# Attention and long-convolution kernel: projection tails in row halves, q begun with the second token quarter, x spectra by thirds

## The chip, the cores and the metric

The kernel runs on one NeuronCore of a Trainium2 chip. Its engines are TensorE (PE; its weight loads are PEld), VectorE (DVE), ScalarE (ACT), GpSimd (POOL) and SyncE (SP), which here only starts DMA transfers. The metric is the device time of one execution in microseconds (us); lower is better. Time before: 226.44 us, the median of 3 runs (225.37 to 228.72).

## What is computed

Two independent blocks whose results stand side by side in the last dimension of the output; S is 2048 tokens, D is 576.

```python
# A: 32 heads of 18, each token looks at 8 keys: itself and those 2, 4, ... 14 tokens back
q, k, v = split(x @ wqkv)
logits = sum_d q[s] * k[s - 2 w] / sqrt(18)      # w = 0..7, masked below token 0
a = (softmax(logits) weighted sum of v[s - 2 w]) @ wo
# B: a short and a long convolution along the tokens, gated
k_shift = 4-tap causal convolution of k with shift_k
kv = k_shift * v
y = causal convolution of kv with ssm_k (length 2048, by FFT) + kv * ssm_D
b = q * y
out = concatenate([a, b], -1)
```

## The kernel before

All operations are put in a list under short names, with a function that issues each one. A long text, ORDER, gives each operation's place in the program and, for those that need it, one of four accumulator slots of 1024 columns. Each engine works off its own instructions in that order, and so do the DMA queues of SP, ACT and POOL. Nothing is reordered at run time: an instruction that waits holds up all that its engine has behind it.

Block A. `load_x` brings x in four token quarters, turned so that channels lie on partitions: `x0`, `x2`, `x3` (channels 0 to 511, in four blocks of 128) and `xt0`, `xt2`, `xt3` (the last 64 channels) by a transposing DMA on SP (L187). Quarter 1 is loaded plainly (`xn`), turned on PE (`nx0` to `nx2`, L299) and copied out (`nx0e`, `nx1e` on ACT, L304; `nx2e` on VectorE, L305). `load_w` brings the weights of q, k and v (comp 0, 1, 2): `w0` to `w2`, four blocks of 128 rows, and `wt0` to `wt2`, the last 64 rows, which lie on partitions 64 to 127 under 64 rows of zeros that `constants` writes (L205). `hot0` and `hot1` are warm-up products (L313).

`project` makes unit `p{comp}{ct}{hh}`: component, channel tile 0 to 4 and token half hh. For q and k with ct below 4 a unit is ten full 128x128 products of 512 columns at L402: two token quarters by five row blocks, the fifth being the 64 rows and the 64 zeros. For v each product is split in two column halves that run side by side, ten pairs. The last tile (ct 4, 64 channels, L415) is five pairs. Each unit's result is copied by ACT (`...e`, L406 or L419).

Behind that come the logits products on VectorE (`l{hh}{ug}{ct}`, L442), their sums over a head on PE with 32-column pieces (`L...`, L450), the softmax (`sm...`; its Exp on ACT, L473), copies of the weights to the heads' channels by DMA on SP (`s...`, `spread`), products with v on VectorE (`w...`, L675) and their sums on PE with 32x32 pieces (`a...`, L689), and the output projection (`o...`, L735), stored by SP.

Block B. `tab...` and `sin0` to `sin3` make tables of sines (L260 to L263, after small number ranges that POOL writes in `constants`); `taps` makes the short convolution with 64x64 pieces on PE, four at a time (L501), `fold` transposes its result, and `x_spectrum(i)` makes the spectra of block i of four: units `x{i}{gi}{pm}`, L547 and L548, evicted at L616. `filter_spectrum` (`k...`, same lines, evicted at L601) does so for the filter. VectorE adds the x spectra's two parts (`S{i}`, L769) and the filter's (`W{d}`, L766), multiplies spectra (`z{j}{t}{i}`, L780), PE sums the products with 32x32 pieces (`Z...`, L804, evicted at L815 or L819), transforms back (`i{j}{t}`, L837, evicted at L841), and `gate` multiplies with q of block B (`g...`, L856, L857, L866, L870) and stores.

The order of PE's units in ORDER, from the warm-up on, up to the first unit of the second token half:

```
hot0 nx0 nx2 nx1 hot1 p030 p000 p100 p110 p010 p020 p120 L000 ti0 p130 L010 p140 p040 L011 L001 L002 p001
```

and around the start of the last part: `p231 p221 p211` are the last value projections; behind `i00`, the first transform back, three x units of block 2 and all eight of block 3 still follow.

Of the kernel before, what the change touches and what calls it, by code (L numbers as in the profile page):

```python
# [16 lines left out]
ORDER = """
1o o 1u 6 u 1c 1i 16 30 5o 4i 36 20 0 2p 120 2e 26 2u 13 2i 3u 3i 8c 5c 6o bl 3c 86 4u 8i 5i 7i 60
9k 66 6c 7o 6i 6u 3o 9u 7u bo 7c al c a0 5u 9o 1k6 a6 ao 126 i mo 56 ax ac 80 mc b6 b0 50 8o n0 ml
40 8w bv 90 nc bc mw c0 ci no 130 go c7 co ni cc cu n6 oc nu d0 d7 46 136 o0 du dc 4o oo 4c o6 e0 oi  # L20
dj pi p0 ou do po 96 16i wu p6 9c gv pc e6 146 h0 pu h6 ek q6 16o qc 13c wi ec 12p m0 eo 12c hf qi
12u 15c 70 12i iw hi 14c 17c ic j0 ho hv 76 16u ii f9 l6 io 1eu 15i qo qu eu i0 r0 176 i6 j6 17i jp
fc r6 fk rc ju ri ro f0 lu 13v fo wo x3 140 x6 je g7 ji 14i xi xc gc 13k 1fj 13o gi lo 17o xu 15o xo
1fo 14q y6 y0 14u kd 180 li k2 ki yi yc k6 fv 152 g0 yu yo lc 156 kp 18i 1f2 ku l0 18c z6 18o z0 1f6
zc zo 170 167 zi 15w 17u zu 16c so 100 1fu tp su 160 ru 1gl 190 t0 s0 186 1h0 18u 106 1go 10c 1jq
10i 1h6 10o 1hi 1g0 1hc tu 10u m6 u0 1m6 t9 1ju 110 u7 1g6 116 s8 tc 1mi 2i0 ti 1k0 1ho 1gc 1mc sc
1fc 1m0 uc ui si 19v 1hu 11c 1d3 11i 198 1d6 v0 19c ur 1a0 11o 11u vq uu vd 1mo 1l6 vu 1l0 1j9 1kc
1q6 1mu 1q0 1iq 1pu 1jc vi 1ji 1n0 1gu 1i9 v6 1iu 1n6 23o 1ic 1oc 25q 1o6 261 23u 1ii w3 1oi 266 1no
1i0 1oo 25u 1nc 1j0 w6 wc 1nx 1ni 1aw 1o0 23c 1b0 24p 1al 23i 1ce 24u 1a6 1p0 1ao 1cp 1ci 253 1ac
1c2 256 19i 1p6 1e0 1c6 273 1b6 1cu 27q 1qc 276 26p 1lc 1pc 27u 1e9 26u 1de 1ec 27d 1di 1br 1ou 27i  # L30
25e 1bu 1bd 25i 1qi 1bi 1s0 1pk 19o 1ku 1li 1lo 24c 1qo 1po 1ki 281 1ko 1si 1s6 286 1ek 1r0 1sc 243
24i 26d 1eo 1do 26i 1ze 1du 1qu 1zv 1zi 1zo 28e 200 20u 1ri 28i 206 246 1lu 20d 2io 210 1r8 20i 216
2n0 21d 1rc 1su 22c 1rq 22i 1so 21i 22o 20o 1tp 1ru 1u0 1tu 293 1t0 1vo 2ae 1u6 21o 21v 296 2ai 29r
1t6 220 1vw 29u 28p 1w0 29c 2mu 1te 28u 29i 2ii 1uo 1ti 1ud 2iu 1uu 2jo 2j2 1ui 2j6 2ki 2ju 2n6 2k0
1v2 2no 22x 1v6 2p0 2ko 230 2oi 2ku 2ne 2ni 2nu 2jc 2qc 1y7 2o0 2ji 2a2 1vf 1yc 1vi 2oo 2ou 2a6 2k9
2p6 1xk 2kc 2pc 1wu 1xv 1x0 2l3 1xo 1y0 1wk 2l6 1w6 1yi 1x7 1wc 2lc 226 2br 1xc 236 2b0 2so 2bu 2bd
2b6 1z3 2ic 2t0 2bi 1yo 1wo 2pj 2pu 1yu 1z6 2ao 2vi 2c2 2au 2cf 2i6 2c6 2o6 2su 2ci 2po 2q2 2zc 2tu
2q6 2oc 2cp 2qi 2uo 2e0 2cu 2tc 2de 2qo 2el 2di 2e6 2d2 2eo 2ec 2t6 2li 2d6 2ti 2to 2v0 2dq 2u0 2f3
2uu 2u6 2f6 2wc 2v6 2du 2fc 2vc 2eu 2qx 2wo 2vo 2gk 2x6 2r0 2vu 2lo 2lu 2r6 2m9 2g1 2m0 2mc 2ro 2zi
2mi 2fl 2g6 2go 2gc 2ru 2ud 2fo 2zu 2fu 2wk 2ui 2wu 2x0 2zo 2xc 30c 300 306 2s2 2xi 2hl 2rc 30i 2s6  # L40
2ri 30o 330 2h2 2ho 30u 2w3 2h6 32i 310 2hc 2sc 2xq 2mo 316 356 32c 2xu 32o 2w6 32u 336 2si 33c 35o
2hu 352 33i 35c 35i 2yu 2y0 35u 360 2y6 33p 366 2z0 2yc 2gu 31c 2yi 33u 31i 36e 2yo 31o 340 2z6 34i
346 36i 31v 34o 34c q0 378 36o 34u 36u 37c 370 320 37i 326
"""


# [35 lines left out]
def kernel(  # L82
# [114 lines left out]
    def constants():  # L197
        nc.vector.memset(pib[:], float(np.float32(np.pi)))
        act(warm[:], pib[:], ACT.Sin)
        nc.gpsimd.iota(rp_i[:, 0:2], pattern=[[128, 2]], base=0, channel_multiplier=1)  # L200
        nc.gpsimd.iota(rp_i[:, 2:4], pattern=[[256, 2]], base=1, channel_multiplier=2)
        for gi in range(4):
            nc.gpsimd.iota(fr_i[:, gi, :], pattern=[[16, 128]], base=4 * gi + 1, channel_multiplier=0)
# [186 lines left out]
    def project(comp, ct, hh):  # L390
        o, pad = ((qat, 0), (kat, PAD), (vat, PAD))[comp]
        o = o(ct, hh)
        box = Box()
        nm = f"p{comp}{ct}{hh}"
        if ct < 4:
            def unit():
                for jp in range(2):
                    for kb in range(5):
                        ws = wcol(comp, kb, ct)
                        for a, w in enumerate(ws):  # L400
                            p = slice(64 * a, 64 * a + 64) if len(ws) > 1 else slice(0, 128)
                            mm(box.ps[p, jp, :], w, xT(kb, 1024 * hh + 512 * (jp ^ a), 512), start=(kb == 0),  # L402
                               stop=(kb == 4), tile_position=(0, 64 * a))

            op(nm, unit, box, 1)
            op(nm + "e", lambda: act(M(o + pad, [[KH if comp == 2 else 512, 2], [1, 512]]), box.ps, ACT.Copy), box,  # L406
               free=True)
# [4 lines left out]
        def unit():
            for kb in range(5):
                for e in range(2):
                    mm(box.ps[64 * e:64 * e + 64, 0, :], wcol(comp, kb, 4)[0], xT(kb, 1024 * hh + 512 * e, 512),  # L415
                       start=(kb == 0), stop=(kb == 4), tile_position=(0, 64 * e))

        op(nm, unit, box, 1)
        op(nm + "e", lambda: act(M1(o + pad, 512), box.ps[:, 0, :], ACT.Copy), box, free=True)  # L419
        if comp:  # L420
            dma(nm + "a", M1(o, PAD)[64:128], M1(o + 512, PAD)[0:64])
# [181 lines left out]
            scale=KSC), box, free=True)  # L603

    def x_spectrum(i):
        for gi in range(4):
            for pm in range(2):
                box = Box()

                def unit(box=box, gi=gi, pm=pm):  # L610
# [4 lines left out]
                op(f"x{i}{gi}{pm}", unit, box, 1)  # L615
                op(f"x{i}{gi}{pm}e", lambda box=box, gi=gi, pm=pm: act(  # L616
                    M((BS if pm else AS) + SPB * i + TH * gi, [[4 * TH, 3], [1, TH]]), acc3(box.ps), ACT.Copy),
                   box, free=True)
# [331 lines left out]
```

## Time and profile before

| | |
|---|---|
| median of 3 runs | 226.44 us (225.37 to 228.72) |
| profiled execution | 226.6 us |
| its span, first to last instruction | 224.9 us |
| mean granted TensorE clock | 0.973 |
| PE busy | 205.2 us, 3027 products |
| VectorE busy | 178.3 us |
| ACT busy | 144.8 us |
| POOL busy | 45.9 us |

In lines of the profile, L402 is line 402 of the kernel before; `<-` stands between what is written and what is read, with partitions x elements; `[5.04 <-X]` is idle time of the engine just before, and what ended it. The large buffer in SBUF is called mem, the accumulator PS. The chain of waits is followed back from the last instruction; "issue" in it is waiting that no semaphore explains. Matmuls are pipelined, so the length of a chain piece divided by its products is their true pitch, while the mean duration of one product is longer.

### The profile page before, as it was taken

The numbers are of one execution on the slowest core, as the hardware profiler recorded it, in microseconds if no ns is written. First come the engines' busy times: TensorE is split into PE (matmuls) and PEld (weight loads), VectorE is DVE, ScalarE is ACT, GpSimd is POOL, SyncE is SP. The second block draws the span as 40 slices with busy tenths as digits, with TensorE's granted clock in tenths as the row PEclk, the third lists the DMA queues.
The fourth block names the chain that finished last, engine by engine and source line by source line (L and its number), as shares of the span: only waits on it lengthen the run. The fifth ranks groups of instructions, "written<-read, shape, count | busy, mean of one in ns | idle before, by whom it ended". The sixth has DMA issues, their size and how long they took to land.

```text
span 224.9 us, 6868 instructions
## 1 busy us (share of the span) xinstructions
PE 205.2 (91%) x3027; PEld 132.9 (59%) x3033; DVE 178.3 (79%) x147; ACT 144.8 (64%) x188; POOL 45.9 (20%) x108
## 2 busy tenths in 40 slices
PE   7379999999999999999999989996899999999590
PEld 3124444445455557678767657663687778787380
DVE  0693787988879967899749999999508999999642
ACT  2322776378794765645989876769998985645140
POOL 7929203001401084020660000000110111010000
PEclk9958999999999999999999999999999999999978
DMA  6999923569894986475541464100666749659323
GB/s 179 292 259 244 176 65 66 82 140 134 157 240 85 190 152 119 75 166 137 130 106 22 112 139 141 55 26 3 212 118 187 245 99 210 218 129 272 125 81 79
DMA packets 54150, 31.87 MB, mean 142 GB/s; under 512 B 41984, under 2 KB 51016, under 8 KB 54120
## 3 DMA queue, kind: packets, MB, share of 16 engines
q1 hardware_dynamic: 50456, 24.12, 46.9%
q0 software_dynamic: 2528, 6.06, 13.2%
q10 hardware_dynamic: 1136, 1.25, 2.0%
q8 instruction: 24, 0.39, 0.8%
q14 instruction: 6, 0.05, 0.1%
HBM read 5.68 MB, written 4.72 MB: 46 GB/s over the span
## 4 chain that ended last, share of the span: by engine, by line
PE 72%; DMA 10%; DVE 5%; ACT 5%; issue 3%; SPq 2%; DVEq 0%; ACTq 0%
PE PS L402 22%; PE PS L735 8%; PE PS L837 8%; PE PS L804 5%; PE PS L547 5%; DMA mem<-in_A_x_dram 5%; PE PS L450 5%; DMA mem<-mem 4%; PE PS L501 3%; PE PS L415 3%; DVE mem L675 3%; PE PS L548 2%; PE PS L689 2%; SPq L184 2%; PE PS L866 2%
## 5 line engine op out<-in xcount | busy, mean ns | idle before, releaser
L402 PE MATMUL PS<-mem 128*64 128x512 bf16 (+1 forms) x314 | 56.7, 392 | 5.4 <-DMA mem<-in_A_x_dram 5.0
L402 PEld LDWEIGHTS <-mem 128*128 128x128 bf16 (+1 forms) x320 | 31.1, 147 | 29.4 <-issue 11.0
L442 DVE TENSOR_TENSOR mem<-mem 128x4096 bf16<-128x4096 bf16 (+1 forms) x20 | 40.6, 2076 | 9.1 <-ACT mem L406 5.7
L675 DVE TENSOR_TENSOR mem<-mem 128x4096 bf16<-128x4096 bf16 x18 | 40.1, 2288 | 4.7 <-DMA mem<-mem 2.9
L406 ACT ACTIVATE mem<-PS 128x1024 bf16<-128x1024 f32 x24 | 24.3, 1023 | 25.3 <-PE PS L402 25.2
L780 DVE TENSOR_TENSOR mem<-mem 128x4608 bf16<-128x4608 bf16 (+3 forms) x21 | 38.1, 1868 | 1.1 <-PE PS L804 0.7
L184 POOL DMA_DIRECT2D mem<-mem x16 | 14.0, 996 | 114.5 <-ACT mem L815 61.0
L547 PE MATMUL PS<-mem 128*128 128x384 bf16 x128 | 33.4, 326 | 2.0 <-ACT mem L695 1.0
L548 PE MATMUL PS<-mem 128*128 128x192 bf16 x128 | 31.4, 246 | 0.0
L735 PE MATMUL PS<-mem 128*128 128x288 bf16 x160 | 21.7, 286 | 0.2 <-DMA mem<-in_A_wo_dram 0.2
L616 ACT ACTIVATE mem<-PS 128x576 bf16<-128x576 f32 x32 | 19.7, 661 | 0.9 <-PE PS L548 0.7
L601 ACT ACTIVATE mem<-PS 128x576 bf16<-128x576 f32 x32 | 19.7, 675 | 0.6 <-PE PS L548 0.2
L837 PE MATMUL PS<-mem 128*128 128x192 bf16 x192 | 18.8, 256 | 0.5 <-ACT mem L819 0.5
L804 PE MATMUL PS<-mem 32*32 32x384 bf16 x960 | 15.1, 328 | 3.9 <-issue 2.6
L547 PEld LDWEIGHTS <-mem 128*128 128x128 bf16 x128 | 12.5, 98 | 9.8 <-issue 1.4
L735 PEld LDWEIGHTS <-mem 128*128 128x128 bf16 x160 | 15.3, 98 | 4.7 <-issue 0.9
L837 PEld LDWEIGHTS <-mem 128*128 128x128 bf16 x192 | 16.8, 102 | 1.9 <-ACT mem L819 0.7
L740 ACT ACTIVATE mem<-PS 128x576 bf16<-128x576 f32 x16 | 10.2, 649 | 8.6 <-PE PS L735 7.7
L804 PEld LDWEIGHTS <-mem 32*32 32x32 bf16 x960 | 9.7, 88 | 9.0 <-issue 6.8
L509 DVE TENSOR_TENSOR mem<-PS,mem 128x512 bf16<-128x512 f32 (+1 forms) x20 | 11.7, 631 | 3.5 <-ACT mem L456 2.1
L548 PEld LDWEIGHTS <-mem 128*128 128x128 bf16 x128 | 12.5, 98 | 2.6 <-issue 1.9
L841 ACT ACTIVATE mem<-PS 128x768 bf16<-128x768 f32 x12 | 9.6, 817 | 5.9 <-PE PS L837 5.8
(111 smaller groups left out, 276.2 us busy)
## 6 DMA issues: line engine op xcount, KB each, us to landing
mem<-mem SPq DMA_DIRECT2D x16, 256.0 KB, 4.3
mem<-mem POOLq DMA_DIRECT2D x8, 288.0 KB, 4.0
out_dram<-mem SPq DMA_DIRECT2D x16, 144.0 KB, 2.3
mem<-mem SPq DMA_DIRECT2D x6, 384.0 KB, 3.4
mem<-mem POOLq DMA_DIRECT2D x6, 384.0 KB, 4.3
mem<-in_B_q_dram SPq DMA_DIRECT2D x4, 576.0 KB, 4.1
out_dram<-mem SPq DMA_DIRECT2D x6, 288.0 KB, 2.5
mem<-in_A_wqkv_dram POOLq DMA_DIRECT2D x2, 576.0 KB, 6.2
```

What stands on the lines that cost most here:

```text
L402: mm(box.ps[p, jp, :], w, xT(kb, 1024 * hh + 512 * (jp ^ a), 512), start=(kb == 0), stop=(kb == 4), tile_position=(0, 64 * a))
L406: op(nm + "e", lambda: act(M(o + pad, [[KH if comp == 2 else 512, 2], [1, 512]]), box.ps, ACT.Copy), box, free=True)
L442: op(f"l{hh}{ug}{ct}", lambda prod=prod, nt=nt, qo=qo, ko=ko, ug=ug: tt(M(prod, [[nt, 4], [1, nt]]), M(qo, [[0, 4], [1, nt]]), M(ko + 2 + ...
L547: mm(view(ps, 0, [[320, 2], [1, TH]]), w, rhs[:, 0:2, :], start=start, stop=stop)
L548: mm(view(ps, 640, [[1, TH]]), w, rhs[:, 2, :], start=start, stop=stop)
L601: op(f"k{m}{gi}{cs}e", lambda: act(M((VS if cs else US) + SPB * (3 - m) + TH * gi, [[4 * TH, 3], [1, TH]]), acc3(box.ps), ACT.Copy, scale= ...
L616: op(f"x{i}{gi}{pm}e", lambda box=box, gi=gi, pm=pm: act(M((BS if pm else AS) + SPB * i + TH * gi, [[4 * TH, 3], [1, TH]]), acc3(box.ps), ...
L675: op(f"w{n}{ct}", lambda: tt(M(P, [[2048, 2], [256, W], [1, 256]]), M(XB[n], [[2048, 2], [256, W], [1, 256]]), M(vo + 2, [[256, 2], [2, W] ...
L735: mm(box.ps[:, h, 0:HD], M1(lhs, 128), M1(rhs, HD), start=(i == 0), stop=(i == 4))
L780: tt(M(pr + 768 * k, [[2304, n], [768, m], [1, 768]]), M(BS + i * SPB + o + PL * k, [[SPB, n], [PL, m], [1, 768]]), M(VS + (3 - j + i) * S ...
L804: mm(view(box.ps[32 * c:32 * c + 32], box.step * (r // 2) + 512 * (r % 2), [[TH, 2], [1, TH]]), I32S[w][32 * r:32 * r + 32], M(pr + src + ...
L837: mm(box.ps[:, pm, TH * c:TH * c + TH], M1(TI + 512 * sl + 256 * pm + 128 * c, 128), M1((YT if j else YRS[0]) + 1536 * t + 768 * pm + TH * ...
```

## The change

Four things change, and ORDER is written anew with them.

1. **Tails.** The last 64 rows of the projection weights are loaded twice, to partitions 0 to 63 (`wt`) and 64 to 127 (`wu`), which adds three DMAs of 72 KB; the zeros and the memset that wrote them are gone. The last 64 channels of x lie on partitions 0 to 63 for token quarters 0 and 2 and on 64 to 127 for 1 and 3. The fifth row block of a unit is then computed by 64-row products, those of two quarters at the same time in the two row halves of the array. In q units and even v tiles the tail comes last, in k units and odd v tiles first.
2. **q first.** Each q unit of the first token half with ct below 4 is cut in two: `p0{ct}0q` makes the four full products of quarter 1, the rest makes those of quarter 0 and the tail.
3. **x spectra.** Unit `x{i}{t}{pm}` makes one third (192) of the channels for all four frequency groups, eight products of 192 columns, evicted as 128x768; before, a unit made one frequency group for all channels, two products of 384 and two of 192 columns, evicted as 128x576. 24 units instead of 32.
4. **Order.** Behind `i00` one x unit of block 2 and all six of block 3 follow. PE's units up to the second token half now are:

```
hot0 nx2 nx0 nx1 hot1 p000q p010q p030q p020q p030 p010 p000 p100 p020 p110 p040 p140 L000 L010 p120 p130 ti0 L001 L011 p001
```

Transposing DMAs on SP were `xt0 x0 vbt0 hl0 kt0 xt3 x2 k0 x3 xt2 va0` and are `xt0 x0 xt3 xt2 vb0 vat0 x3 hl0 x2 k0`. ACT's first steps were the DMAs `xn wt0 w0`, the Sin table with a small warm-up (in `const0`), `nx0e nx1e`; they are the DMAs `xn w0 wu0 wt0`, then `nx1e`, `const0`'s table and warm-up, `nx0e`. POOL's DMAs were `w1 wt2 wt1`, then the ranges of `const0`, `sh4 sh0 w2`; they are `wu1 w1 wt1 sh4 sh0`, then the ranges; `wu2 w2` stand behind `p001`'s issue and `wt2` after the first taps. ACT's use of tables was `sin0 sin2 sin3 sin1 sm0x sm1x` and is `sin3 sin2 sin0 sm0x sin1 sm1x`. On VectorE, `S2` and `z201` now stand ahead of `g00h`. On SP, `s300` now stands behind the store `o0000s`.

The diff, without ORDER:

```diff
@@ constants
-        nc.gpsimd.memset(M(WW + 4 * D, [[5 * D, 3], [1, D]])[0:64], 0.0)
@@ load_w
-        dma(f"wt{comp}", M1(b + 4 * D, D)[64:128], A_wqkv[512:576, comp * D:(comp + 1) * D], eng)
+        for a in range(2):
+            dma(f"w{'tu'[a]}{comp}", M1(b + 4 * D, D)[64 * a:64 * a + 64], A_wqkv[512:576, comp * D:(comp + 1) * D], eng)
@@ load_x
-        xbar(f"xt{qtr}", M1(X4 + 512 * qtr, 512), xf[512 * qtr:512 * qtr + 512, 448:576])
+        xbar(f"xt{qtr}", M1(X4 + 512 * qtr, 512),
+             bass.AP(tensor=xf.tensor, offset=xf.offset + 512 * qtr * D + (448 if qtr % 2 else 512), ap=[[D, 512], [1, 128]]))
@@ project
+        cols = (0,) if comp < 2 and ct < 4 else (0, 1)
+        jps = (0, 1) if ct < 4 else (0,)
+        tail_first = (comp == 1) if comp < 2 else ct % 2 == 1
+        two = comp == 0 and hh == 0 and ct < 4
+        def full(jp, first, last):
+            for kb in range(4):
+                ws = wcol(comp, kb, ct)
+                for a in cols:
+                    p = slice(64 * a, 64 * a + 64) if len(cols) > 1 else slice(0, 128)
+                    mm(box.ps[p, jp, :], ws[a % len(ws)], xT(kb, 1024 * hh + 512 * (jp ^ a), 512),
+                       start=first and kb == 0, stop=last and kb == 3, tile_position=(0, 64 * a))
+        def tails(first):
+            ws = wcol(comp, 4, ct)
+            for jp in jps:
+                for a in cols:
+                    r = jp ^ a
+                    p = slice(64 * a, 64 * a + 64) if len(cols) > 1 else slice(0, 128)
+                    mm(box.ps[p, jp, :], ws[a % len(ws)][64 * r:64 * r + 64],
+                       xT(4, 1024 * hh + 512 * r, 512)[64 * r:64 * r + 64], start=first, stop=not first,
+                       tile_position=(64 * r, 64 * a))
+        def unit():
+            if tail_first:
+                tails(True)
+            for jp in jps[:1] if two else jps:
+                full(jp, not tail_first, tail_first)
+            if not tail_first:
+                tails(False)
+        if two:
+            op(nm + "q", lambda: full(1, True, False), box, 1)
+        op(nm, unit, box, 0 if two else 1)
@@ x_spectrum
-        for gi in range(4):
+        for t in range(3):
             for pm in range(2):
...
-                    for c in range(2):
-                        mm3(box.ps, M1(TX + 1024 * c + 512 * pm + 128 * gi, 128),
-                            thirds(AB + 2304 * i + 1152 * c + 576 * pm), c == 0, c == 1)
+                    for gi in range(4):
+                        for c in range(2):
+                            mm(box.ps[:, gi // 2, TH * (gi % 2):TH * (gi % 2) + TH],
+                               M1(TX + 1024 * c + 512 * pm + 128 * gi, 128),
+                               M1(AB + 2304 * i + 1152 * c + 576 * pm + TH * t, TH), start=(c == 0), stop=(c == 1))
```

More of the change, by code (lines that the diff above doesn't have):

```diff
@@ L23 @@
[L23 to L27, printed above, removed]
@@ new lines @@
+wk w0 1mi 1kd 1mo 1r0 1oc 1lu 1lo 1jx 1ki wo 1nu 1jd 1k0 1ec 1k6 1o0 24u 1ji 1pc x9 1pi 26k 250 1jo
+1po 1ou xc 1j6 1pu 1oi xi 1ko 26o 1lc 1p2 1oo 1c3 1p6 24i 1c6 1d8 24o 25v 279 1dc 1bc 260 1q6 268
+1bi 1ap 26c 1di 1cc 27c 1dw 1q0 1mc 1f6 1do 1br 1rc 1au 27i 1ri 1e0 1cj 1qc 27o 1fe 1co 27u 1fi 287
+1qi 280 1cw 1bu 1ei 1d0 1eo 1ro 1qq 1to 28c 1m6 1mu 1m0 25j 1qu 1s0 1ti 26u 1l6 1tc 270 1ew 1s6 259
+1f0 1fo 20k 1fu 25c 1ru 210 20o 21l 20u 216 1t6 1so 220 21o 25o 21u 1se 1n0 226 2h6 21c 22c 1v6 1si
@@ L44 @@
+35u 35i 30i 360 30o
 """
@@ L394, in project @@
         nm = f"p{comp}{ct}{hh}"
-        if ct < 4:
[L396 to L405, printed above, removed]
+        cols = (0,) if comp < 2 and ct < 4 else (0, 1)
[28 more added lines that the diff above has]
+        op(nm, unit, box, 0 if two else 1)
+        if ct < 4:
             op(nm + "e", lambda: act(M(o + pad, [[KH if comp == 2 else 512, 2], [1, 512]]), box.ps, ACT.Copy), box,
@@ L410, in project @@
             return
[L412 to L418, printed above, removed]
         op(nm + "e", lambda: act(M1(o + pad, 512), box.ps[:, 0, :], ACT.Copy), box, free=True)
@@ L605, in x_spectrum, with unit @@
     def x_spectrum(i):
-        for gi in range(4):
+        for t in range(3):
             for pm in range(2):
                 box = Box()
-                def unit(box=box, gi=gi, pm=pm):
-                    for c in range(2):
-                        mm3(box.ps, M1(TX + 1024 * c + 512 * pm + 128 * gi, 128),
-                            thirds(AB + 2304 * i + 1152 * c + 576 * pm), c == 0, c == 1)
[L615 to L618, printed above, removed]
+                def unit(box=box, t=t, pm=pm):
+                    for gi in range(4):
[3 more added lines that the diff above has]
+                               M1(AB + 2304 * i + 1152 * c + 576 * pm + TH * t, TH), start=(c == 0), stop=(c == 1))
+                op(f"x{i}{t}{pm}", unit, box, 1)
+                op(f"x{i}{t}{pm}e", lambda box=box, t=t, pm=pm: act(
+                    M((BS if pm else AS) + SPB * i + 4 * TH * t, [[2 * TH, 2], [1, 2 * TH]]), box.ps[:, :, 0:2 * TH],
+                    ACT.Copy), box, free=True)
     taps(0)
```

41 lines of the change are left out of this document (20 added, 21 removed).

## The prediction

> **What bounds the kernel now.** I read the page from its head to the chain, then the table by stretches, then the order of time at the start, then the chain's pieces.
>
> ```profile
> span 224.9 us, 6868 instructions
> PE 205.2 (91%) x3027; PEld 132.9 (59%) x3033; DVE 178.3 (79%) x147; ACT 144.8 (64%) x188; POOL 45.9 (20%) x108
> PE 72%; DMA 10%; DVE 5%; ACT 5%; issue 3%; SPq 2%; DVEq 0%; ACTq 0%
> ```
>
> PE carries 72% of the chain, but not everywhere. The table by stretches (stretch, length, busy us and instruction counts of PE, PEld, DVE, ACT, POOL, then clock, DMA share, GB/s):
>
> ```profile
> 140.00:150.00 10.00, 9.80 (x102) 6.62 (x103) 10.00 (x5) 8.19 (x13) 0.00 (x0) 1.00 0.14 46
> 150.00:160.00 10.00, 7.68 (x310) 4.84 (x278) 9.14 (x8) 8.69 (x13) 0.00 (x0) 1.00 0.23 78
> 160.00:170.00 10.00, 9.69 (x151) 8.01 (x152) 2.03 (x3) 9.31 (x14) 1.77 (x2) 1.00 0.54 124
> 8.00:12.90 4.90, 0.02 (x1) 0.12 (x2) 4.74 (x7) 0.00 (x0) 3.78 (x6) 0.84 1.20 294
> 12.90:18.20 5.30, 5.25 (x12) 1.85 (x13) 5.25 (x9) 2.01 (x2) 2.15 (x4) 0.51 1.22 285
> ```
>
> From 140 to 160 VectorE is full and PE has slack; from 160 PE leads again. At the start PE is idle for 4.9 us and then works 5.3 us at half clock. The order of time there:
>
> ```profile
> 1.29 1.18 ACTq L184 DMA_DIRECT2D mem<-in_A_wqkv_dram  x2
> 2.50 1.28 ACT L199 ACT_TABLE_LOAD   x1 [2.50 <-issue]
> 3.80 0.20 ACT L199 ACTIVATE warm<-pib 128x1 f32<-128x1 f32 x1
> 5.48 1.94 ACT L304 ACTIVATE mem<-PS 128x1024 bf16<-128x1024 f32 x2 [1.48 <-PE PS L299]
> 5.95 1.89 PE L313 MATMUL PS<-mem 128*128 128x512 bf16 x8
> 8.48 0.10 PEld L402 LDWEIGHTS <-mem 128*128 128x128 bf16 x1 [1.14 <-DMA mem<-in_A_wqkv_dram]
> 12.88 17.84 PE L402 MATMUL PS<-mem 128*128 128x512 bf16 x68 [5.04 <-DMA mem<-in_A_x_dram]
> 24.09 6.70 DVE L442 TENSOR_TENSOR mem<-mem 128x4096 bf16<-128x4096 bf16 x3 [5.13 <-ACT mem L406]
> ```
>
> The q weights are there at 8.48 and token quarter 1 (turned on PE, evicted at L304) at 7.42; PE waits until 12.88 for quarter 0, which the DMA transposes. VectorE's first logits product waits for its operands until 24.09.
>
> **The change, part by part.** Lengths of chain pieces (start, us, what):
>
> ```profile
> 12.88 5.28 PE PS L402 x12
> 47.73 0.99 PE PS L501 x16
> 86.35 2.37 PE PS L402 x20
> 88.71 2.16 PE PS L415 x20
> 109.85 0.27 PE PS L547
> 111.16 5.62 DMA mem<-mem
> 161.81 0.16 PE PS L547
> 162.05 0.16 PE PS L547
> 200.77 3.96 PE PS L837 x48
> ```
>
> A turn of 512 columns takes 0.44 us cold (5.28/12) and 0.216 warm (2.16/10, since 20 half-width products run in pairs).
>
> *q with the second quarter.* The four new q pieces need 16 turns, the q weights and quarter 1, and not the transposed quarter 0. Their start is set by ACT. It issues one DMA more ahead of its first eviction, which is free (1.29 + 3 x 0.59 = 3.06, before hot1 begins at 5.95, behind the transposes), but in the new order the constants, with the Sin table, stand between the two evictions of quarter 1: 5.95 + 0.2 + 1.0 + 1.28 + 0.20 + 1.0 = 9.6 (1.0 is half of L304's two; 0.2 and a further 0.1 are handovers). So q begins near 9.75 (bounds 8.48, when weights came, and 12.88). If warm, 16 turns end at 9.75 + 3.45 = 13.2, when quarter 0 has just come: PE's useful work begins 3.1 us earlier, and the 12 turns that ran at 0.44 run at 0.216: 12 x 0.22 = 2.7 more. Gain 5.8.
>
> Does VectorE follow? Its tables wait for POOL's iotas, which now stand behind five DMA issues of POOL (the extra weight rows among them; W2's loads moved far back):
>
> ```profile
> 5.22 2.08 POOL L184 DMA_DIRECT2D mem<-in_A_wqkv_dram  x3
> 7.42 0.86 POOL L203 IOTA mem<- 128x128 int32 x4
> 9.64 1.39 POOL L184 DMA_DIRECT2D sh<-in_B_shift_k_dram  x2
> 9.92 2.11 DVE L260 TENSOR_SCALAR mem<-mem,rp 128x512 int32<-128x512 int32 x3
> 15.98 2.98 DVE L335 TENSOR_TENSOR mem<-mem,sh 64x1280 bf16<-64x1280 bf16 x2
> ```
>
> 5.22 + 2.08 + 1.39 + about 1.0 of iotas = 9.7; then the tables and the diagonals, which took 9.92 to 18.96 here and have one step more (2.11/3 = 0.7): 19.5. The memset that is removed stood behind the iotas and sets nothing. PE's operands for the first product: 13.2, then p030, p010, p000, p100 with 24 turns (5.2) and six changes of tile shape (0.8), and an eviction of 1.0: 20.2. So products begin near 20.3 instead of 24.09, 3.8 earlier, and VectorE's own idle places behind it give the rest; PE needs the second product 0.6 before it is there. I charge +0.6.
>
> *Tails in row halves.* 16 q/k units go from ten turns to nine and 8 v units from ten pairs to nine, if the halves run side by side; the five-turn units of the last channels keep five. 24 x 0.216 = 5.2 saved. Against it stand changes of tile shape: counted unit by unit in the two orders, PE passes 71 before and 104 after, since the new order puts a q unit that ends in a tail ahead of a k unit that begins with one. Price: the taps' 16 products (L501) are four turns, 0.86, and took 0.99, so 0.13 for a group; 20 half-width products took 2.37 after another shape and 2.16 beside their own, 0.21 for both ends of a group. 33 x 0.13 = 4.3. Net -0.9. Row halves on the full width have no row; the nearest are the same taps, 64x64 pieces four at a time, of which two share each column half from different row halves: 16 products in 0.99, so row halves do run together. Bounds: -5.2 if changes cost nothing; +4.3 if the halves ran one after the other. I take -0.9, by the row nearest in shape. The Trainium skill (TensorEngine Tiling, Key Properties) says that changing the tiling mode drains TensorE; the 0.13 agrees. By that page's twofold speedup alone, without the drain, the term would be -5.2 and the time some 4 lower.
>
> All this lies ahead of the last value projection (109.85). There the chain goes on by the spread of the attention weights (DMA 5.62) into VectorE, whose work from there to i00 is the same: the gain is handed on, neither more nor less. One transfer of the last spread now stands behind an output store on SP's queue, so the fourth group of products could wait: 0 to 2, I take 0.5.
>
> *x spectra in thirds.* PE before: 32 units of two pairs, a pair each 0.245 (162.05 - 161.81): 15.7. After: 192 products of 192 columns at 3.96/48 = 0.0825: 15.8. Weight loads rise by 128:
>
> ```profile
> L616 ACT ACTIVATE mem<-PS 128x576 bf16<-128x576 f32 x32 | 19.7, 661 | 0.9 <-PE PS L548 0.7
> L841 ACT ACTIVATE mem<-PS 128x768 bf16<-128x768 f32 x12 | 9.6, 817 | 5.9 <-PE PS L837 5.8
> ```
>
> They are hidden: PE loads weights for nearly each product (x3033 beside x3027), those of L837 too, and these run at 0.0825. ACT: 32 x 0.661 = 21.2 becomes 24 x 0.817 = 19.6, not on the chain. What counts is where the units stand: behind i00, where PE leads, the old order has 11 of them (5.4), the new one seven (4.6): -0.8. S2 and a product of j=2 move ahead of the gate on which VectorE idles between 160 and 170; PE leads there, so zero.
>
> *Table.* sin1 now stands between the two Exp calls, so ACT loads two tables more, 1.28 each. The first falls while PE has four tap units and two projections in hand, the second while VectorE evicts taps: 0, or 2.6 if PE or VectorE stood waiting for ACT instead.
>
> Sum: -5.8 + 0.6 - 0.9 + 0.5 - 0.8 = -6.4. The profiled execution took 226.6 (span 224.9 and 1.7 around it), the median is 226.44, so both stand for the same state: 226.6 - 6.4 = **220.2**.
>
> **The rivals.**
>
> *Cold clock (222.9).* PE is idle from 7.84 to 9.75. Near the end a 2.57 us stop was followed by half clock:
>
> ```profile
> 211.13 0.37 PE L804 MATMUL PS<-mem 32*32 32x384 bf16 x12 [2.57 <-issue]
> 213.13 2.74 PE L837 MATMUL PS<-mem 128*128 128x192 bf16 x16
> 216.37 1.48 PE L837 MATMUL PS<-mem 128*128 128x192 bf16 x16
> ```
>
> If 1.9 us is enough too, q's first turns cost 0.44 again and the 2.7 is lost. Against it: warm-up matmuls end only 1.9 before. The Trainium skill (TensorE: Matmul & The Clock Gate, Part 1) has a free-running window of 3413 ns that must be idle; by that rule 1.9 us never cools it and the time is 220.2. The trace differs in part: here 2.57 us did cool it.
>
> *Halves in turn (225.4).* The tails save no turn but still change shape: +5.2. For it: no row of full-width halves. Against it: the taps.
>
> *The end's stop goes (216.4).* The 2.57 stop, which no semaphore ended, and the slow spectrum behind it (2.74 - 1.48) fall away, since other transfers meet PE's instruction stream there: -3.8. For it: the order of the last q loads and products differs. Against: 128 more instructions to fetch.
>
> *Waits of the new order (224.3).* The late spread and ACT's tables cost their upper bounds, 2 and 2.6: 1.5 and 2.6 more than charged. For it: VectorE is full from 140 to 160 and passes on any wait. Against: both have other work in front.
>
> *Quarter 2 late: slower (236).* On SP's queue x2 now comes behind xt3, xt2, vb0, vat0, x3 and hl0; quarter 0's issue ends at 7.99.
>
> ```profile
> 8.04 1.26 SPq L187 DMA_TRANSPOSE mem<-in_B_v_dram  x1
> 9.34 1.36 SPq L187 DMA_TRANSPOSE mem<-in_B_ssm_k_dram  x1
> 12.67 4.41 SPq L187 DMA_TRANSPOSE mem<-in_A_x_dram  x2
> 24.86 3.02 SPq L187 DMA_TRANSPOSE mem<-in_B_v_dram  x1
> mem<-in_A_x_dram SPq DMA_TRANSPOSE x6, 6.0
> ```
>
> Back to back: 7.99 (just ahead of the row at 8.04) + 2 x 4.41 + 3.02 + 1.26 + 1.36 = 22.5, and 6.0 to landing: 28.5. PE wants it (p001) 91 turns (19.7) and 18 changes of shape (2.3) after 9.75, and the 0.6: 32.4. Each us past 32.4 costs one; past 38.8 the change is slower than before. If each transpose waited for the landing of the one before, seven of them at 5 (quarter 0 took 12.88 - 7.99) would land x2 near 48 and cost 16: 236 (12.88 + 7 x 5 = 48). Against it: the issues above follow each other at once.
>
> **How the numbers follow.** Forecast (217.5 to 221.9) 0.46; end's stop gone 0.12; cold clock 0.16; halves in turn 0.10; waits 0.08; quarter 2 late 0.08. The range 215.5 to 226 leaves out the last and a little on each side; the forecast's own is 217.5 to 222. Under 2%, some 4.5 us, is about what a measurement of this kernel cannot tell from no change. Faster by more: 0.46 + 0.12 = 0.58. Within: 0.16 + 0.10 + 0.08 = 0.34. Slower: 0.08.
>
> **What would show it.** q's first product at 9.75 and no half clock behind it; VectorE's first product near 20.3; 64-row products starting in pairs; the last value projection ending near 103.7 instead of 109.85; from there to i00 as long as before; x evictions x24 near 0.8. Wrong: q's start past 11, half clock, p001 waiting for a DMA, PE idle between p211 and i00 by over 2 more.

## The result and the profile after

The changed kernel takes 228.9 us (median of 20 runs, 225.53 to 232.08). The kernel before took 225.53 us in runs on the same chips (20 runs, 223.35 to 228.72). The ratio is 1.0122, with a 95% interval of 1.0077 to 1.0168: the change costs 1.2%, where 220.2 us had been forecast. (The ratio leaves disturbed runs of both kernels out, so here and below it isn't the quotient of the two medians.) Where two kernels are compared below, the difference is that of their ratios, in parts of 225.5 us. The profiled execution of the changed kernel took 231.59 us, 2.7 more than the median, so lengths from it lie on the high side.

From the page of the changed kernel: the busy time of each engine, and the chain of waits by engine.

```profile
PE 206.6 (90%) x3091; PEld 133.1 (58%) x3097; DVE 177.8 (77%) x147; ACT 148.3 (65%) x183; POOL 57.8 (25%) x109
PE 55%; POOL 9%; DMA 9%; ACT 8%; SPq 7%; issue 7%; DVE 2%; DVEq 0%; POOLq 0%; ACTq 0%
```

PE, VectorE and ACT are busy about as long as before. POOL is busy for 11.9 us more (57.8 instead of 45.9), with one instruction more, and it holds 9% of the chain, where it did not appear before. So the same POOL instructions have become longer, and something waits for them. The waits of the changed kernel (engine and what it writes, what it waited for, us in total, times, longest) name them:

```profile
POOL mem L184 <- DMA mem<-in_B_ssm_k_dram: 11.8, 1, 11.8
ACT mem L597 <- POOL mem L449: 6.8, 1, 6.8
PE PS L363 <- ACT mem L433: 4.2, 1, 4.2
```

None of the three stood in the profile before. The pieces of the chain from 16.8 to 44.3 us (start, length, what) put them in one line; left out between them are waiting that no semaphore explains, POOL's other constants and its memory clears:

```profile
16.82 4.21 DMA mem<-in_B_ssm_k_dram
...
21.32 0.88 POOL mem L184
...
36.37 2.25 POOL mem L250
...
38.71 2.36 POOL mem L449
...
41.09 1.16 ACT mem L597
42.25 0.92 ACT mem L433
...
43.22 1.04 PE PS L363 x32
```

Read from the top: `hl0` (L187) is the transposing DMA that brings a part of the long filter, B_ssm_k. The new order issues it eighth on SP's queue instead of fourth, and it lands at 21.03. `hd` (L184) is a DMA on POOL's queue that adds the row B_ssm_D to what `hl0` brought. It waits 11.77 us for that landing, and POOL works in order, so everything behind `hd` waits too: the mirrors `mirr` (L231), the constants `const2` (L243 to L250) and `kpad` (L449), which copies a margin of k. ACT's `hn0` (L597), which negates another part of the filter, writes over a place that `kpad` still reads. It therefore waits 6.78 us, and on ACT the evictions of `p001` and `p011` (L433) stand behind it. With these two accumulators still full, PE has none for `ti1` (L363), and stops for 4.17 us.

Why is POOL so late? Its own order of time, first in the kernel before:

```profile
17.75 1.37 POOL L232 TENSOR_SCALAR_AFFINE_SELECT mem<-mem 128x128 bf16<-128x128 bf16 x1
...
20.65 0.90 POOL L184 DMA_DIRECT2D mem<-in_B_ssm_D_dram  x1
21.23 0.62 POOL L244 COPY mem<-mem 128x128 bf16<-128x128 bf16 x1
21.51 0.89 POOL L245 TENSOR_SCALAR mem<-mem 128x128 bf16<-128x128 bf16 x1
22.78 1.37 POOL L251 TENSOR_SCALAR_AFFINE_SELECT mem<-mem 32x128 bf16<-32x128 bf16 x4
35.17 1.86 POOL L430 COPY mem<-mem 128x64 bf16<-128x64 bf16 x1 [11.03 <-ACT mem L406]
```

and the same instructions in the changed kernel:

```profile
21.32 0.88 POOL L184 DMA_DIRECT2D mem<-in_B_ssm_D_dram  x1 [11.77 <-DMA mem<-in_B_ssm_k_dram]
22.48 2.35 POOL L231 TENSOR_SCALAR_AFFINE_SELECT mem<-mem 128x128 bf16<-128x128 bf16 x1
25.38 1.75 POOL L243 COPY mem<-mem 128x128 bf16<-128x128 bf16 x1
27.11 2.56 POOL L244 TENSOR_SCALAR mem<-mem 128x128 bf16<-128x128 bf16 x1
29.68 0.29 POOL L247 MEMSET mem<- 128x32 bf16 x4
30.05 8.58 POOL L250 TENSOR_SCALAR_AFFINE_SELECT mem<-mem 32x128 bf16<-32x128 bf16 x4
38.69 2.37 POOL L449 COPY mem<-mem 128x64 bf16<-128x64 bf16 x1
```

Before, all of them but `kpad` were done by 24.15, when VectorE's logits products had just begun (24.09). Now they run from 22.48 on, beside a VectorE that multiplies without a pause. `hd` itself begins only 0.67 later than before (21.32 instead of 20.65). Two other things have moved: `mirr` stands behind `hd` now instead of ahead of it, and VectorE's products begin 1.70 earlier:

```profile
22.39 16.06 DVE L461 TENSOR_TENSOR mem<-mem 128x4096 bf16<-128x4096 bf16 x7 [4.01 <-ACT mem L433]
```

Seven products in 16.06 us are 2.29 each. The POOL instructions that read the memory now take 1.75 to 2.56 each, however small they are: the four selects go from 1.37 to 8.58, 2.15 each, the copy from 0.62 to 1.75. The memsets at L247, which read nothing, take 0.29 for four, no more than before. The Trainium skill (SBUF — State Buffer, Who interferes with whom) says that a VectorE instruction with two inputs in SBUF contends with a GpSimd instruction that reads SBUF, because its second input comes through a read interface that both share, and not with one that only writes. The trace agrees in both halves: 2.15 beside products of 2.29, and memsets of 0.07.

What the stop costs is seen in the stretch from 40 to 50 us, first before, then after (length, busy us and counts of PE, PEld, DVE, ACT, POOL, then clock, DMA share, GB/s):

```profile
40.00:50.00 10.00, 9.95 (x117) 4.23 (x116) 9.40 (x7) 5.73 (x6) 0.00 (x0) 1.00 0.47 101
```

```profile
40.00:50.00 10.00, 6.45 (x65) 2.52 (x66) 4.59 (x5) 4.01 (x4) 2.44 (x3) 0.66 0.64 148
```

PE loses 3.5 us of busy time, and part of the rest runs at half clock, which brings the mean to 0.66: 65 products instead of 117. VectorE falls from 9.40 to 4.59, since it gets no operands.

The start of the changed kernel went the other way, but less than forecast:

```profile
5.40 1.28 ACT L306 ACT_TABLE_LOAD   x1 [5.40 <-DMA mem<-in_A_x_dram]
...
7.72 1.28 ACT L199 ACT_TABLE_LOAD   x1
...
10.18 4.11 PE L407 MATMUL PS<-mem 128*128 128x512 bf16 x12 [2.25 <-ACT mem L306]
```

q begins at 10.18, and its twelve products run in 4.11, 0.34 each instead of 0.216, because the granted clock falls to half at 11.4 and comes back at 14.8. VectorE's first product is at 22.39 instead of 24.09. At the first sums of logits 3.7 us were won (26.98 instead of 30.65); at the end of the last value projection 4.9 were lost (114.70 instead of 109.85).

### The profile page after: what moved, and what is told of

Its sections match the earlier page's. It is cut to its first block, busy times and chain, and to the rows that moved or that the text cites. A ratio compares the mean times of both kernels' runs of the same rounds, so it can differ in the third digit from the quotient of the medians.

```text
span 229.8 us, 7003 instructions
## 1 busy us (share of the span) xinstructions
PE 206.6 (90%) x3091; PEld 133.1 (58%) x3097; DVE 177.8 (77%) x147; ACT 148.3 (65%) x183; POOL 57.8 (25%) x109
## 4 chain that ended last, share of the span: by engine, by line
PE 55%; POOL 9%; DMA 9%; ACT 8%; SPq 7%; issue 7%; DVE 2%; DVEq 0%; POOLq 0%; ACTq 0%
PE PS L407 9%; PE PS L756 8%; SPq L187 7%; PE PS L632 6%; PE PS L858 5%; PE PS L825 4%; PE PS L566 4%; PE PS L710 4%; POOL mem L250 3%; DMA mem<-mem 3%; DMA mem<-in_A_wqkv_dram 3%; PE PS L520 3%; PE PS L417 2%; ACT mem L840 2%; PE PS L567 2%
## 5 line engine op out<-in xcount | busy, mean ns | idle before, releaser
L407 PE MATMUL PS<-mem 128*64 128x512 bf16 (+1 forms) x298 | 53.5, 394 | 3.1 <-ACT mem L306 2.2
L461 DVE TENSOR_TENSOR mem<-mem 128x4096 bf16<-128x4096 bf16 (+1 forms) x20 | 41.1, 2101 | 16.6 <-PE PS L469 9.6
L433 ACT ACTIVATE mem<-PS 128x1024 bf16<-128x1024 f32 x24 | 24.2, 1022 | 28.8 <-PE PS L407 17.0
L407 PEld LDWEIGHTS <-mem 128*64 128x64 bf16 (+1 forms) x304 | 26.9, 146 | 26.0 <-issue 13.8
L184 POOL DMA_DIRECT2D mem<-mem x16 | 13.9, 1006 | 111.6 <-ACT mem L836 62.7
L756 PE MATMUL PS<-mem 128*128 128x288 bf16 x160 | 22.6, 296 | 0.7 <-issue 0.7
L637 ACT ACTIVATE mem<-PS 128x768 bf16<-128x768 f32 x24 | 19.0, 814 | 3.3 <-PE PS L632 3.2
L620 ACT ACTIVATE mem<-PS 128x576 bf16<-128x576 f32 x32 | 20.0, 659 | 1.7 <-PE PS L567 1.5
L566 PE MATMUL PS<-mem 128*128 128x384 bf16 x64 | 18.1, 332 | 2.4 <-DMA mem<-mem 0.9
L756 PEld LDWEIGHTS <-mem 128*128 128x128 bf16 x160 | 15.9, 101 | 5.6 <-issue 1.4
L632 PE MATMUL PS<-mem 128*128 128x192 bf16 x192 | 18.6, 246 | 0.0
L858 PE MATMUL PS<-mem 128*128 128x192 bf16 x192 | 17.5, 246 | 0.5 <-ACT mem L840 0.5
L632 PEld LDWEIGHTS <-mem 128*128 128x128 bf16 x192 | 16.0, 98 | 1.5 <-issue 0.7
L858 PEld LDWEIGHTS <-mem 128*128 128x128 bf16 x192 | 16.0, 98 | 1.2 <-issue 0.8
L761 ACT ACTIVATE mem<-PS 128x576 bf16<-128x576 f32 x16 | 10.4, 652 | 9.4 <-PE PS L756 6.8
L567 PE MATMUL PS<-mem 128*128 128x192 bf16 x64 | 15.9, 250 | 0.0
L390 POOL COPY mem<-mem 64x16 bf16<-64x16 bf16 x24 | 10.3, 427 | 16.6 <-ACT mem L433 15.6
```

What stands on the lines that cost most here:

```text
L407: mm(box.ps[p, jp, :], ws[a % len(ws)], xT(kb, 1024 * hh + 512 * (jp ^ a), 512), start=first and kb == 0, stop=last and kb == 3, tile_posi ...
L461: op(f"l{hh}{ug}{ct}", lambda prod=prod, nt=nt, qo=qo, ko=ko, ug=ug: tt(M(prod, [[nt, 4], [1, nt]]), M(qo, [[0, 4], [1, nt]]), M(ko + 2 + ...
L566: mm(view(ps, 0, [[320, 2], [1, TH]]), w, rhs[:, 0:2, :], start=start, stop=stop)
L567: mm(view(ps, 640, [[1, TH]]), w, rhs[:, 2, :], start=start, stop=stop)
L620: op(f"k{m}{gi}{cs}e", lambda: act(M((VS if cs else US) + SPB * (3 - m) + TH * gi, [[4 * TH, 3], [1, TH]]), acc3(box.ps), ACT.Copy, scale= ...
L632: mm(box.ps[:, gi // 2, TH * (gi % 2):TH * (gi % 2) + TH], M1(TX + 1024 * c + 512 * pm + 128 * gi, 128), M1(AB + 2304 * i + 1152 * c + 576 ...
```

## The experiments

Theory P: the wait for `hl0` on POOL's queue, through the late constants, `kpad` and `hn0`, costs the 4 to 7 us that turn a gain into a loss. Rivals: the row halves of the tails (they run in turn, or change shape too often; T in the expectations), ACT's table loads (A there), the x spectra in thirds, or the early q itself. Where an experiment only moves an operation in ORDER, its diff is given as the words of ORDER around it. Most of these kernels have five lines less of ORDER, so a line L250 of the changed kernel is their L245.

### 1. POOL's constants early

The changed kernel with `mirr` and `const2` moved ahead of VectorE's products; `hd` and its wait stay.

```diff
- sh0 nx1e const0 nx0e ... p020e mirr p120 sin2 const2 l011
+ sh0 nx1e const0 mirr const2 nx0e ... p020e p120 sin2 l011
```

> The changed kernel with GpSimd's mirr and const2 moved to right behind const0, ahead of hd's wait for the filter's first rows; nothing else moves. Theory P (GpSimd's small constants fell into VectorE's stream of products, so kpad, then the ACT copy hn0, then two evictions come late): the 4.17 us stop of PE at 43 and the half clock from 40 to 50 go, hn0 no longer waits 6.8 us for GpSimd, and the time falls by 4 to 6, to about 224. Rival T (the row halves cost more in changes of tile shape than they save): no change, 229. Rival A (the second pair of table loads on ACT is the cost): no change, 229.

Measured: 222.22 us (220.81 to 223.5), ratio to the kernel before 0.989 [0.9833, 0.9946]. That is 5.2 less than the changed kernel. POOL, and the wait of `hn0`:

```profile
13.35 2.30 POOL L245 TENSOR_SCALAR_AFFINE_SELECT mem<-mem 32x128 bf16<-32x128 bf16 x4
34.81 1.16 ACT L592 ACTIVATE mem<-mem 128x1152 bf16<-128x1152 bf16 x1 [1.59 <-POOL mem L444]
```

The selects take 2.30 instead of 8.58, `hn0` waits 1.59 instead of 6.78, and PE does not stop there. One caution: q's first products ran at full clock in the profile of this run, and the first sums of logits begin at 25.89 instead of 26.98, so up to 1.1 of the 5.2 may come from the start. One stop of PE is left that the kernel before does not have, 1.29 us behind ACT:

```profile
57.65 0.39 PE L412 MATMUL PS<-mem 64*128 64x512 bf16 x2 [1.29 <-ACT mem L428]
```

### 2. The Sin table's place as well

```diff
- sin0 he0 ... l110 vm0 sin1 k1
+ sin0 sin1 he0 ... l110 vm0 k1
```

> As pool_early, and sin1 moved ahead of sm0x, right behind sin0, so that ACT loads two tables fewer. If A is right as a part, the 1.28 us stop of PE at 65.7 goes too and the time is 1 to 2 below pool_early, about 222.5; if the loads are covered, it is the same as pool_early. P alone: 224. T: 229.

Measured: 220.27 us (219.47 to 222.11), 0.982 [0.9758, 0.9882], 1.6 less than experiment 1. The intervals of the two overlap, but the 1.29 stop is gone. So the table loads for a `sin1` between the two Exp calls were not hidden: PE stood waiting for ACT.

### 3. The same wait put into the kernel before

The kernel before, with `hl0` issued behind `k0`, and `mirr` behind `hd`.

```diff
- const0 nx2 hl0 nx1 ... p110 mirr p100e ... hd const2
+ const0 nx2 nx1 ... k0 hl0 ... p110 p100e ... hd mirr const2
```

> The kernel before with hl0 moved behind k0 on SyncE's queue, and hd, mirr and const2 in this order, so that these constants meet VectorE's products as in the changed kernel. Theory P: the four affine selects of const2 take 8 us instead of 1.4, hn0 waits for kpad, PE stops for some 4 us near 42, and the time rises by 3 to 6 to about 230. T and A: within 1 of before, 225.5.

Measured: 227.78 us (224.79 to 233.84), 1.0079 [1.0026, 1.0131], 1.8 more than before. The direction is that of theory P, the size below what was expected, and the path another one (`hd` begins at 26.50, even later than the 21.32 of the changed kernel):

```profile
26.50 0.89 POOL L179 DMA_DIRECT2D mem<-in_B_ssm_D_dram  x1 [8.00 <-DMA mem<-in_B_ssm_k_dram]
...
33.06 1.04 PE L356 MATMUL PS<-mem 128*32 128x128 bf16 x31 [3.04 <-POOL mem L240]
33.39 1.35 POOL L246 TENSOR_SCALAR_AFFINE_SELECT mem<-mem 32x128 bf16<-32x128 bf16 x4
```

Here PE waits 3.04 us for `const2`'s matrix itself (L240), since `ti0` comes earlier in this order. That stop leaves VectorE without operands, and the selects behind it take 1.35 for four: without a product beside them they are as short as they were.

### 4. Only `hn0` later

POOL is left as late as in the changed kernel; only ACT's `hn0` goes behind the evictions.

```diff
- va0 p011 hn0 l003 p001e ... L013 p101e L014
+ va0 p011 l003 p001e ... L013 p101e hn0 L014
```

> The changed kernel with one ACT step moved: hn0 behind p101e, so that ACT's evictions p001e and p011e do not stand behind it; GpSimd's constants stay late. If the stop of PE at 43 comes by way of ACT's queue (kpad late, hn0 waits, two evictions behind hn0, no free accumulator), the 4.2 us stop goes although the constants are as late as before, and the time falls by 3 to 6 to 223 to 226. If GpSimd's lateness reaches PE by another way as well (VectorE slowed, the 32-column table), the time falls by less than 2.

Measured: 223.49 us (221.45 to 225.54), 0.990 [0.9843, 0.9957], 5.0 less than the changed kernel. POOL's selects and `kpad` are as long as there, and the stretch from 40 to 50 is whole again:

```profile
28.95 8.57 POOL L245 TENSOR_SCALAR_AFFINE_SELECT mem<-mem 32x128 bf16<-32x128 bf16 x4
37.59 2.37 POOL L444 COPY mem<-mem 128x64 bf16<-128x64 bf16 x1
```

```profile
40.00:50.00 10.00, 9.57 (x80) 4.21 (x80) 8.42 (x10) 7.99 (x10) 1.35 (x2) 1.00 0.68 156
```

This is the cleanest test of the path. POOL's constants meet VectorE's products as in the changed kernel, and that alone costs little; it is ACT's queue, with `hn0` ahead of two evictions, that carries the delay to PE. One caution: q's first products ran at full clock in the profile of this run, everything there is 1.1 earlier (the first sums of logits begin at 25.88, in the changed kernel's profile at 26.98), and up to 1.1 of the 5.0 may come from that.

### 5. Without the row halves

The tails as whole 128-row products with 64 rows of zeros, as in the kernel before, in the order of the changed one. The three added weight DMAs go with the halves, and the memset of the zeros is back. Nothing is left out of the computation.

```diff
-                    mm(box.ps[p, jp, :], ws[a % len(ws)][64 * r:64 * r + 64],
-                       xT(4, 1024 * hh + 512 * r, 512)[64 * r:64 * r + 64], start=first, stop=not first,
-                       tile_position=(64 * r, 64 * a))
+                    mm(box.ps[p, jp, :], ws[a % len(ws)], xT(4, 1024 * hh + 512 * r, 512), start=first,
+                       stop=not first, tile_position=(0, 64 * a))
```

> The changed kernel with its order, but the fifth row block as before: 128 rows with 64 of zeros, tails as full products, one weight load of these rows and the memset again. Theory P: the stop at 43 stays, and the time moves by at most 1.5 either way, 228 to 230 (24 turns more, some 33 changes of tile shape less). T: the time falls by 2 to 4, to 225 to 227.

Measured: 227.49 us (221.81 to 231.97), 0.9934 [0.9857, 1.0012], 4.2 less than the changed kernel. It tells nothing of the halves, because the stop moved with it: `kpad` met no product of VectorE in the profiled run, and PE stopped for 1.83 us instead of 4.17. The comparison was made again without the waits of experiments 1 and 2:

> pool_sin_early (220.3) with the tails as full 128-row products of zeros again, so that the two waits are out of the way and the row halves stand alone. If the prediction's term for them holds (24 turns saved against 33 changes of tile shape), the time rises by 0.5 to 1.5, to about 221. Rival T (changes cost more than the turns): it falls by 1 to 3, to 218 or so. If changes were free: it rises by 5, to 225.

Measured: 221.99 us (219.05 to 224.9), 0.9863 [0.9759, 0.9967], against 220.27 and 0.982 with the halves. It is confounded again: here PE stops for 2.07 us for the last 64 rows of v's weights, whose DMA (`wt2`) the new order issues only after the first taps.

Experiments 9 and 10 make the comparison without these stops.

### 6. Whole q units

The kernel of experiment 2 without q's early part:

```diff
-        two = comp == 0 and hh == 0 and ct < 4
+        two = False
```

The units `p000q` to `p030q` drop out of ORDER with it.

> pool_sin_early with the four q units whole, at the place of their second parts, so that PE waits for token quarter 0 again. By the prediction's term (3.1 earlier and 2.7 less at half clock) the time rises by 4 to 6, to about 225. If the early start is given back later (a wait on VectorE's or SyncE's side sets the pace until 40), it rises by 2 at most.

Measured: 224.21 us (221.02 to 227.96), 0.9912 [0.9859, 0.9966], 2.1 more than experiment 2, where 4 to 6 were expected; the intervals just overlap (the medians lie 3.9 apart). PE then waits 4.61 us for quarter 0:

```profile
13.47 3.13 PE L402 MATMUL PS<-mem 128*128 128x512 bf16 x7 [4.61 <-DMA mem<-in_A_x_dram]
```

So the early q is no cause of the loss; it is worth about 2 us.

### 7. The Sin table ahead of the evictions

The kernel of experiment 2 with `const0` ahead, so that ACT loads its table while it waits for x:

```diff
- w1 xt3 wt1 nx2 nx0 sh4 nx2e nx1 hot1 sh0 nx1e const0 mirr const2 nx0e
+ w1 xt3 wt1 const0 nx2 nx0 sh4 nx2e nx1 hot1 sh0 mirr const2 nx1e nx0e
```

> pool_sin_early with const0, and so the Sin table on ACT, ahead of both evictions of quarter 1. If ACT's order is what holds q's start at 10.7, the 1.8 us stop of PE ahead of it shrinks to 0.5, the half clock behind it may go too, and the time falls by 1 to 2.5 to about 218.5. If the start is set by q's weights, no change.

Measured: 218.51 us (217.85 to 220.86), 0.9786 [0.970, 0.9872], 0.8 less than experiment 2, which is within the noise.

```profile
5.43 1.28 ACT L194 ACT_TABLE_LOAD   x1 [5.43 <-DMA mem<-in_A_x_dram]
8.80 4.48 PE L402 MATMUL PS<-mem 128*128 128x512 bf16 x20 [0.69 <-ACT mem L301]
```

ACT loads one table instead of two, q begins 1.4 us earlier than in the changed kernel, and twenty products run in 4.48, at full clock.

### 8. Thirds alone

The kernel before with the x spectra made in thirds, the units of the fourth frequency group dropped from ORDER (they have no work left).

```diff
-        for gi in range(4):
+        for t in range(3):
```

> The kernel before with x spectra in thirds alone: its first three units of each half block stand for the thirds, the fourth is left out, all else as before. By the prediction's working PE is 0.2 longer and ACT 1.6 shorter off the chain, with 0 to 0.8 gained where PE leads: within 1 of before, 225. If 192-column products were held by their weight loads, the time would rise by 3 or more.

Measured: 226.91 us (223.68 to 230.04), 1.0067 [1.0007, 1.0127], 1.5 slower, where a change of up to 1 either way was expected. The evictions are as forecast (24 of 0.820), but an order that was made for 32 units does not fit 24: PE waits 1.58 us for an accumulator in one place.

```profile
178.99 0.83 PE L607 MATMUL PS<-mem 128*128 128x192 bf16 x8 [1.58 <-ACT mem L811]
```

### 9 and 10. All of it early, with and without the row halves

Experiment 7 with `wt2` issued right behind `w2`, so that no weights are late; then the same with whole 128-row tails.

```diff
- l012 p140a w2 va0 p011 ... sm0h t04h wt2 t02l
+ l012 p140a w2 wt2 va0 p011 ... sm0h t04h t02l
```

> table_first (218.5) with the last weight rows of v (wt2) loaded right behind w2. In some of the kernels PE stood 0.5 to 2 us for them; in table_first it did not. Expected: 218 to 218.5, no more than 0.5 below table_first.

> all_early with the tails as full 128-row products of zeros: the row halves alone, now without the late weight rows that stopped PE for 2.07 us in fixed_no_halves. By the prediction's term the time is 0.5 to 1.5 above all_early; if changes of tile shape cost more than the turns saved, it is below all_early.

Measured: 219.49 us (217.28 to 221.11), 0.9718 [0.9658, 0.9779], with the halves; 218.72 us (218.16 to 220.51), 0.9735 [0.9686, 0.9784], without. The two cannot be told apart: the ratios allow the halves to be some 2 us better or 1.5 worse. In the profile with halves PE also waits 0.89 us for quarter 0, and without them it does not. The chain's pieces show why the halves bring so little; with halves, then without:

```profile
14.59 0.97 PE PS L402 x4
15.55 0.32 PE PS L412 x2
```

```profile
13.67 0.86 PE PS L400 x4
14.54 0.43 PE PS L410 x2
```

Four whole products and the tails of two quarters take 0.97 + 0.32 = 1.29 with halves, and 0.86 + 0.43 = 1.29 without. The halves do run side by side: the 0.32 is one turn of 0.216 and a change of tile shape (the way PE splits its array for a product) of 0.11, where whole products need two turns. But the change back costs 0.11 as well (0.97 - 0.86). In a unit that stands alone the two changes are as long as the one turn of 0.216 that was saved. Only where two tails stand side by side is something left: from the first tail to the end of `L010` it is 11.68 with halves and 11.98 without.

Both kernels are faster than the kernel before and than the changed one. The intervals of experiments 7, 9 and 10 overlap, so none of the three is shown to be the best.

## Why the prediction was wrong

**The step that failed** is the one on POOL. The prediction followed POOL's queue only as far as the number ranges, which VectorE's tables need ("they now stand behind five DMA issues of POOL"), and it noted that `x2` comes behind `hl0` on SP's queue, without asking who waits for `hl0`. It should have followed each moved transfer to its readers: `hl0` has one on POOL, `hd`, and behind that reader stood `mirr`, `const2` and `kpad`. Nor did it ask what VectorE's earlier products would meet: by its own 20.3 for their start, `const2` at its old place (21.23 to 24.15) would already have run beside them. Two rows of before gave the price: `kpad` took 1.86 for 64 columns beside a product, and `mirr`'s select 1.37 beside the diagonals, where it takes 0.29 in experiment 1. The term was put at nothing; experiments 1 and 4 put it at 5.2 and 5.0 us, of which up to 1.1 may belong to the start. Without it the changed kernel would have been faster than before, by about 1%. Theory P holds, and what carries the delay to PE is shown for ACT's queue (experiment 4).

**q with the second quarter**, forecast -5.8: about 2 (experiment 6), so this term was too large by more than half. q began at 10.18, not 9.75: with the added weight DMA, called free, ACT's issues ran until 5.37 instead of 3.06 (in experiment 10, without it, until 2.39), and the first copy makes ACT load a table of its own (5.40) ahead of the Sin table (7.72), a second load of 1.28 that the prediction did not count. The rival *Cold clock* came true in the profiled execution: after 2.25 us of idle time the clock fell to half, and the products took 0.34 on average. In the profiles of experiments 1, 2 and 4 PE was idle for 1.80 us, and the clock stayed whole; the last section has what tells the two cases apart. For VectorE's first product the forecast said 20.3; it was 22.39, and 21.30 with the whole clock of experiment 1.

**Table**, forecast 0 with an upper end of 2.6: 1.6 (experiment 2). The cover named for the first load was "four tap units and two projections in hand"; PE had the work, but no accumulator for it, since the evictions stood behind the table on ACT. In the changed kernel the two rows are

```profile
62.32 1.28 ACT L262 ACT_TABLE_LOAD   x1
65.72 0.39 PE L417 MATMUL PS<-mem 64*128 64x512 bf16 x2 [1.28 <-ACT mem L433]
```

**Tails**, forecast -0.9: no difference that can be measured (experiments 9 and 10), which does not exclude the -0.9. Side by side was right, and 0.11 for a change beside the 0.13 that was taken. At -5.2, the bound for changes that cost nothing, experiment 9 would have been 5 us faster than experiment 10, and it was not. The rival *Halves in turn* is excluded by the 0.32.

**x spectra**, forecast -0.8: on the order of before they cost 0.7% (experiment 8). What they are worth in the new order was not tried. The sizes were right, 24 evictions of 0.814.

```profile
L637 ACT ACTIVATE mem<-PS 128x768 bf16<-128x768 f32 x24 | 19.0, 814 | 3.3 <-PE PS L632 3.2
```

**From the last value projection to `i00`**, forecast equal but for 0.5 of a late spread. The stretch of before, of the changed kernel, and of experiment 2:

```profile
109.85:160.31 50.46, 46.05 (x934) 31.83 (x933) 46.19 (x25) 41.73 (x64) 4.99 (x12) 1.00 0.37 92
```

```profile
114.70:167.36 52.66, 47.84 (x986) 36.25 (x985) 44.53 (x25) 42.72 (x60) 6.27 (x17) 0.97 0.37 94
```

```profile
104.30:155.53 51.23, 46.07 (x987) 35.44 (x985) 43.63 (x25) 42.68 (x59) 6.06 (x17) 1.00 0.37 96
```

52.7 and 51.2 instead of 50.5: 2.2 and 0.8 us longer, around the bounds of 0 to 2. In the changed kernel the clock is at half for 3.4 us of this stretch (its mean is 0.97), and VectorE waits for the spread of weights for 6.4 us in all, before for 2.9; the longest of these waits:

```profile
121.84 8.90 DVE L696 TENSOR_TENSOR mem<-mem 128x4096 bf16<-128x4096 bf16 x4 [4.63 <-DMA mem<-mem]
```

**The other rivals.** *The end's stop goes* did not come true. Where the kernel before has one such stop of 2.57 us, the changed one has four between 189 and 221, of 0.92, 0.73, 0.72 and 0.65, 3.0 together; the first:

```profile
189.51 0.53 PE L825 MATMUL PS<-mem 32*32 32x384 bf16 x26 [0.92 <-issue]
```

*Quarter 2 late* did not either: no product waits for that DMA. *Waits of the new order* named ACT's tables rightly and missed the larger wait.

**How the sum stands.** With both waits taken out the kernel runs in 220.27 us, next to the 220.2 forecast. That is luck in part, and no proof of the terms: the forecast counts from 226.44, while the kernel before took 225.1 in runs beside this one, and the ratio of 0.982 is a gain of 4.1 us where 6.4 were forecast. The early q gave over 3 less than forecast, the tails nothing that can be measured, the thirds were not tried in this order, and the order as a whole gave something that no experiment here assigns. What the experiments do settle is that the two waits, 5.2 and 1.6, are what lies between a loss of 1.2% and a gain of 1.8%.

## What to carry to other kernels

When a transfer is moved back in its queue, list its readers, and for each reader list what is queued behind it on its engine, then who waits for that, until the path ends or reaches the engine that bounds the kernel. A small instruction on GpSimd is cheap only at a time when VectorE is not reading two operands, so its place in time is part of its price, and a change that makes VectorE start earlier changes that price too. Before saving a turn of TensorE by a change of tile shape, count the changes that go with it: here two of 0.11 us ate one turn of 0.216 in each unit that stood alone.

## What the hardware showed

- A GpSimd instruction that reads SBUF takes about as long as the VectorE product of two SBUF operands beside it: 2.15 for a select on 32 partitions that takes 0.34 alone. One that only writes isn't lengthened (0.07 for a memset). Beside the table steps of VectorE, which read one operand, the same select takes 0.58 (experiment 1).
- In the 13 profiles TensorE's granted clock changes only at steps of 3.41 us, counted from a start that differs from execution to execution. What the drops follow is how long PE was busy in the step before, not the length of one stop: at full clock, and the ends of the kernels left out, 14 steps with 0 to 1.67 us of busy time were followed by half clock, while two with 1.58 and 1.60 and all with 1.84 or more were not. So whether q starts slowly hangs on where the steps fall, and that differs from execution to execution. Steps of the changed kernel, and the one of experiment 4 that has the stop in it:

```profile
8.00:11.41 3.41, 1.23 (x6) 0.58 (x6) 2.44 (x6) 2.12 (x3) 1.54 (x7) 1.00 1.11 317
11.41:14.82 3.41, 3.19 (x9) 1.22 (x8) 3.38 (x8) 0.00 (x0) 0.00 (x0) 0.50 1.25 226
```

```profile
6.93:10.34 3.41, 2.04 (x13) 0.94 (x12) 1.37 (x3) 3.04 (x4) 2.62 (x9) 1.00 1.19 301
```

  The Trainium skill (TensorE: Matmul & The Clock Gate, Part 1) tells of a window of 3413 ns, free-running, that must be idle. The length and the free phase agree; but here a window in which PE was busy for 1.23 us was enough.
- ACT loads a table for its first copy: the table load at 5.40 in the changed kernel stands ahead of the copy, and with the Sin warm-up ahead the copies need none of their own (one load instead of two, experiment 7).
- A pair of row halves of 64 rows and 512 columns takes 0.32 us with the change of tile shape ahead of it, against 0.43 for two whole products. The change takes 0.11.
- In the last part PE stops without a semaphore, at other places and for other lengths in each kernel. In the profiles of before, of the changed kernel and of experiment 7, all nine such stops end 1.3 to 1.6 us after a 16 KB transfer on an instruction queue (before: the transfer ends at 209.6, PE goes on at 211.13); most of these transfers are followed by no stop. That is an agreement in time, not a cause that was tested.
